# A tile shared by two batches earlier in the order, gates of nine tiles made together, and weight copies behind the exponentials

## The chip, the cores and the metric

The kernel runs on one core of one Trainium2 chip. A core has TensorE (matmuls and transposes), VectorE, ScalarE, GpSimd and SyncE (which here issues most DMAs), each with its own in-order queue of instructions, and they meet by semaphores only. The metric is the device time of one execution in microseconds; lower is better.

## The reference

Three stages follow one another: attention in a sliding window, a mixture of experts with one expert for each token, and a squared-ReLU network.

```python
# attention: q, k, v are (4, 8, 576, 64)
scores = scale * np.matmul(q, k.transpose(0, 1, 3, 2))
rel = pos[:, None] - pos[None, :]
scores = np.where((rel >= 0) & (rel < 64), scores, -1e9)
attn = softmax(scores)                       # exp, sum + 1e-9
x = np.matmul(attn, v)                       # -> (2304, 512): 4 batches of 576 rows
...
# experts: 8, with w1 (8, 512, 1024), w2 (8, 1024, 512)
logits = normalized(x) @ normalized(expert_emb).T / tau
expert_idx = np.argmax(logits, axis=1)
gate_w = softmax(logits)[arange, expert_idx]
out[mask] = gate_w[mask, None] * (np.maximum(x[mask] @ w1[e], 0.0) @ w2[e])
...
# second network: w_in (512, 2048), w_out (2048, 512)
r = np.maximum(x @ w_in, 0.0)
y = (s * (r * r) + b) @ w_out
```

## The kernel before

The 2304 rows of x are 18 tiles of 128, numbered 0 to 17. A batch has 576 rows, four and a half tiles, so tile 4 holds the last half of batch 0 and the first half of batch 1, and tile 13 the same of batches 2 and 3. Heads go in four pairs. A unit is one batch and one pair of heads; unit u = 4 * batch + pair, 16 in all. Q and K of a unit are loaded by SyncE, turned by TensorE in four pieces (K and Q, two heads each; `prep`, L220) and copied by ScalarE (both K pieces and the first Q piece) or VectorE (the second Q piece). There are eight sets of buffers for Q, K and V; unit u + 8 takes those of unit u once no step is left that uses u (`free`, L832).

Attention is 36 steps, numbered 0 to 35 here, in the order of the list `steps` (L825). Most steps take one pair of heads for two neighbouring tiles (`by_pair`); tiles 4 and 13, which lie in two batches, take steps of their own with two pairs of heads each (`alone`), and use four units at once. In the kernel before, tile 4 has steps 12 and 17, behind two pairs of heads of tiles 5 to 8 each time. A step n issues, on all engines in an order written out by hand: the scores (mask and products, TensorE, L251 and L210), the minimum and the subtraction (VectorE, L261 and L263), pieces of Q and K for later steps, the transposes of an earlier step's exponentials (`flip`, L271; two steps back, from step 31 on one), the exponential (ScalarE, L268), and then for a step one further back the product with V and the scaled output rows (`pv`, L279; L286 on TensorE, L289 to L295 on VectorE). How many pieces a step prepares (`prepare`, L885) follows from the units that the coming steps need: three pieces more than needed, less 2.4 for each step between, as far as the buffers are free. When a unit's last piece is turned, Q and K of the unit two further on are loaded, and V of the next as soon as its buffer is free.

When a tile's last pair of heads is done, `fin` (L673) starts its routing. GpSimd squares its rows and adds them up for the norm (`squares`, L399: one instruction over 512 elements and nine that halve; only tiles below 11). Later steps write the tile to DRAM, turn it (`route_turn`), and make its logits. For groups of tiles the table `ROUTED` (L792) then gives due steps, counted from the step of `fin`, for: ranks (`route_rank`, VectorE), count (`route_count`, TensorE), list (`route_list`, VectorE), `part` and `listed` for the tokens' numbers, and for the gates `route_norm` (one GpSimd root, L467), `route_gate` (L469: five VectorE instructions, an Exp on ScalarE, eight VectorE instructions), `part` again (the product Qv, VectorE, L458) and `listed` (one matmul a tile). In the kernel before, the groups are tiles 0 to 3 (gates at step 21), 4 to 8 (step 29) and 9 to 12 (step 32), each with ranks and gates of its own; the gates of the rest come after attention.

Work that is due is put down with `later` and one of four kinds, run in this order within a step (`run`, L808): TURN and WHOLE ahead of the exponential, HALF right behind it, BEHIND after the output rows.

When tiles up to 12 are counted, `first_weights` (L724) reads the number of the first full expert, loads four chunks of its first weight, and puts down a copy of each for steps 33 to 36. Such a copy (`split`, L85) is a rounding of 128 x 1024 on ScalarE (L86) and a difference on GpSimd (L87). `first_turn` (L742) at step 35 scales and turns the gathered rows for that expert. After attention come the experts, a planned order of the other engines around TensorE's fixed one, and the second network.

Of the kernel before, what the change touches and what calls it, by code (L numbers as in the profile page):

```python
# [20 lines left out]
def tile_kernel(ctx, tc, q, k, v, emb, tau, w1, w2, w_in, w_out, s_in, b_in, out, x_dram, y_dram, y0_dram, wi_dram, wo_dram):  # L21
# [14 lines left out]
    TL = 16  # L36
# [172 lines left out]
    def add(out, a, b):  # L209
        nc.tensor.matmul(out, a, b, start=False, stop=True, skip_group_check=True)  # L210
# [68 lines left out]
    def pv(slots, pT):  # L279
        po = ps1.tile([128, 4, D + 1], F32, tag="po", name="po")  # L280
        for s, (t, hp) in enumerate(slots):
            for h in range(2):
                for c in range(2):
                    rows = slice(64 * c, 64 * c + 64)
                    u, i = unit(t, hp, c)
                    nc.tensor.matmul(po[rows, 2 * s + h], pT[:, 2 * s + h, rows], vbufs[u][:, vslot(i), h], start=True, stop=True)  # L286
        with tc.high_priority(offset=PVP):
            rc = at3.tile([128, 4], F32, tag="rc", name="rc")
            nc.vector.tensor_scalar(rc, po[:, :, D], 1e-9, None, op0=ALU.add)  # L289
            nc.vector.reciprocal(rc, rc)  # L290
            (t0, h0), (t1, h1) = slots
            x = xs[t0].rearrange("p s (h q d) -> p s h q d", h=2, q=NP)
            x = x[:, :, :, h0] if t0 != t1 else x[:, 0, :, h0:h0 + 2].rearrange("p h q d -> p q h d")
            v4 = [128, 2, 2, D]
            nc.vector.tensor_tensor(x, po[:, :, :D].rearrange("p (s h) d -> p s h d", h=2),  # L295
                                    rc.rearrange("p (s h) -> p s h", h=2).unsqueeze(3).to_broadcast(v4), op=ALU.mult)
# [81 lines left out]
    def route_turn(t, lp=None):  # L378
        xw = rows_of(t)
        tp = ps3.tile([128, ND, 128], F32, tag="tp", name="tpx")  # L380
        for c in range(ND):
            nc.tensor.transpose(tp[:, c], xw[:, c * 128:(c + 1) * 128], ident)
        xt = (lp or at3).tile([128, ND, 128], F32, tag=f"xt{t}" if lp else "xt", name="xt")
        marks.append(nc.scalar.activation(xt, tp, AF.Copy))
        if t >= LATE:
            sq = (lp or at).tile([128, DM], F32, tag="sq", name="sq")
            if t >= TL:
                nc.vector.tensor_tensor_reduce(out=sq, in0=xw, in1=xw, scale=1.0, scalar=0.0,
                                               op0=ALU.mult, op1=ALU.add, accum_out=ss[:, t:t + 1])
            else:  # L390
                nc.scalar.activation(sq, xw, AF.Square, accum_out=ss[:, t:t + 1])
        return xt
# [6 lines left out]
    def squares(t):  # L399
        sq = x2p.tile([128, 1024], F32, tag="xh", name="sq")[:, :DM]  # L400
        nc.gpsimd.tensor_tensor(sq, rows_of(t), rows_of(t), op=ALU.mult)
        c = DM // 2
        while c >= 1:
            o = ss[:, t:t + 1] if c == 1 else sq[:, :c]
            nc.gpsimd.tensor_tensor(o, sq[:, :c], sq[:, c:2 * c], op=ALU.add)
            c //= 2
# [47 lines left out]
    def part(t0, t1, j0, j1):  # L454
        w, ts_ = j1 - j0, slice(t0, t1)
        vb_ = [128, t1 - t0, w, E * KT]
        Qv = rp2.tile(vb_, BF16, tag=f"Qv{w}", name="Qv")
        nc.vector.tensor_tensor(Qv, Q[:, ts_].rearrange("p t e k -> p t (e k)").unsqueeze(2).to_broadcast(vb_),  # L458
                                val[:, ts_, j0:j1].unsqueeze(3).to_broadcast(vb_), op=ALU.mult)
        return Qv  # L460

    def listed(t0, t1, j0, j1, Qv):
        for t in range(t0, t1):
            add(ls[:, j0:j1], lane[:, t], Qv[:, t - t0])

    def route_norm(t0, t1):
        nc.gpsimd.tensor_tensor(nrm[:, t0:t1], ss[:, t0:t1], half.to_broadcast([128, t1 - t0]), op=ALU.pow)  # L467

    def route_gate(t0, t1):  # L469
        n = t1 - t0  # L470
        ts_ = slice(t0, t1)

        sc = nrm[:, ts_]
        nc.vector.tensor_scalar(sc, sc, 1e-6, None, op0=ALU.add)
        nc.vector.reciprocal(sc, sc)
        scb = sc.unsqueeze(2).to_broadcast([128, n, E])
        L = rp2.tile([128, n, E], F32, tag="L", name="L")
        nc.vector.tensor_tensor(L, logit[:, ts_], scb, op=ALU.mult)
        mx = mxs[:, ts_]
        nc.vector.tensor_tensor(mx, mx, sc, op=ALU.mult)  # L480
        nc.vector.tensor_tensor(L, L, mx.unsqueeze(2).to_broadcast([128, n, E]), op=ALU.subtract)
        nc.scalar.activation(L, L, AF.Exp)
        gt = rp2.tile([128, n], F32, tag="gt", name="gt")
        nc.vector.tensor_reduce(gt, L, axis=AX.X, op=ALU.add)
        nc.vector.tensor_scalar(gt, gt, 1e-9, None, op0=ALU.add)
        nc.vector.reciprocal(gt, gt)
        for j in range(3):
            nc.vector.tensor_copy(val[:, ts_, 2 + j], gt)
            if j < 2:
                nc.vector.tensor_tensor(gt, gt, val[:, ts_, 2 + j], op=ALU.subtract)  # L490
# [182 lines left out]
    def fin(slots, pT):  # L673
        pv(slots, pT)
        t = slots[0][0]
        if slots[-1][1] < NP - 1:
            return
        ts_ = sorted({t for t, _ in slots})
        nt = len(ts_)
        if t < LATE:  # L680
            for k_ in ts_:
                squares(k_)

        def write():
            nc.sync.dma_start(x_dram[t * 128:(t + nt) * 128].rearrange("(s p) n -> p s n", p=128), xs[t])

        n = now[0]
        if n < len(steps):
            later(n + 1, write)
        else:  # L690
            write()
        if t == TL:
            return
        xts = {}

        def turned(t):
            xts[t] = route_turn(t)

        for j, k_ in enumerate(ts_):
            m = n + (0 if t >= LATE else j)  # L700
            later(m + 1, lambda k_=k_: turned(k_), TURN)
            later(m + 2, lambda k_=k_: route_logits(k_, xts[k_]), HALF)
        if ts_[-1] not in ROUTED:
            return
        (t0, t1), d = ROUTED[ts_[-1]]
        q = []
        later(n + d[0], lambda: route_rank(t0, t1), BEHIND)
        later(n + d[1], lambda: route_count(t0, t1))
        if t1 == TF:
            later(n + d[1], first_weights)  # L710
        later(n + d[2], lambda: route_list(t0, t1))
        later(n + d[3], lambda: q.append(part(t0, t1, 0, 2)))
        later(n + d[4], lambda: listed(t0, t1, 0, 2, q[0]))
        if t1 == TL:
            return
        later(n + d[5], lambda: route_norm(t0, t1))
        later(n + d[6], lambda: route_gate(t0, t1), BEHIND)
        later(n + d[7], lambda: q.append(part(t0, t1, 2, 5)), BEHIND)
        later(n + d[8], lambda: listed(t0, t1, 2, 5, q[1]))
        if t1 == TF:  # L720
            later(n + d[9], first_turn)
            later(n + d[4], first_rows)

    def first_weights():  # L724
        route_first(TF)
        rv = nc.values_load(efi[0:1, 0:1], engines=[mybir.EngineType.SP], min_val=0, max_val=E - 1)
        srcs.extend(expert_srcs(rv))
        w = sets[0] = []
        for c in range(ND):
            hl, do = load_part(srcs[c], nc.gpsimd)  # L730
            w.append(hl)
            later(now[0] + 2 + c, do, TURN)
        xa[:] = [x2p.tile([128, ND, 256], F32R, tag=t, name=t) for t in ("xh", "xl")]

    def first_rows():
# [39 lines left out]
    def first_part():  # L775
# [4 lines left out]
        for d in range(ND):  # L780
# [4 lines left out]
            if d == ND - 1:  # L785
# [3 lines left out]
    now = [0]  # L789
    TOACT = (("k", 0), ("k", 1), ("q", 0))  # L790

    ROUTED = {3: ((0, 4), (4, 5, 6, 7, 9, 10, 11, 12, 14)),  # L792
# [3 lines left out]
    LATE = 11  # L796
    xa = []
    xga = []
# [4 lines left out]
    TURN, WHOLE, HALF, BEHIND = range(4)  # L803

    def later(n, do, kind=WHOLE):
        todo.setdefault(n, []).append((kind, do))
# [11 lines left out]
    def by_pair(ts_, hps=range(NP)):  # L818
        return [((t, hp), (t + 1, hp)) for hp in hps for t in ts_]

    def alone(t, hp):
        return [((t, hp), (t, hp + 1))]


    steps = by_pair((0, 2)) + \  # L825
        by_pair((5, 7), (0, 1)) + alone(4, 0) + by_pair((5, 7), (2, 3)) + alone(4, 2) + \
        by_pair((9, 11)) + alone(13, 0) + alone(13, 2) + by_pair((14,)) + by_pair((16,))
    FIRST = {t: s[0][0] for s in steps for t, _ in s}
    used = [[(2 * t + c) // NW * NP + hp for t, hp in s for c in range(2)] for s in steps]
# [122 lines left out]
    with tc.manual_schedule(engines={mybir.EngineType.PE}):  # L952
        some(2)
        xts = [(t, route_turn(t, lp)) for t in range(TL, NTT)]
        with tc.issue_after(marks[-1].ins):
            for src in srcs[ND:]:
                hl, do = load_part(src, nc.gpsimd)
# [362 lines left out]
```

## Time and profile before

| | us |
|---|---|
| median of three runs | 868.21 |
| lowest and highest | 868.17, 868.93 |
| the profiled execution's own time | 870.09 |
| its span, first to last instruction | 868.3 |
| busy in the span: TensorE, VectorE, ScalarE, GpSimd | 791.0, 533.7, 383.3, 214.0 |
| last exponential of attention starts | 171.6 |

The profile is one execution. Its page gives the busy time of each engine, a picture of the span in 40 slices of 21.7 us, the chain that ended last and the costliest groups. Its views of single stretches give a line to each instruction (or run of equal ones): start, length, engine, source line, operation, what it writes and reads, and in brackets how long the engine stood idle before it and what ended that.

### The profile page before, as it was taken

The page shows a single profiled execution, that of the slowest core. Times are in us where ns is not written, and L with a number is a line of the kernel's source. Part 1 is how long each engine was busy: PE and PEld are TensorE (multiplying, and loading weights), DVE is VectorE, ACT ScalarE, POOL GpSimd, SP SyncE. Part 2 cuts the span into 40 slices and gives each one's busy share as a digit, 9 for nine tenths or more (in the row PEclk, how much of TensorE's full clock was granted, in tenths as well). Part 3 has the DMA queues.
Part 4 walks back from the last instruction along what each step waited for, and adds up shares of the span by engine and source line. Part 5 has one row for each costly group of instructions (what it writes and reads, how often), then busy time and mean ns, then how long its engine had stood idle before and what let it go on. Part 6 is the DMA issues. An engine that isn't in the chain of part 4 may idle for free. (4 is left out here: it accounts for less than half of the span.)

```text
span 868.3 us, 16641 instructions
## 1 busy us (share of the span) xinstructions
PE 791.0 (91%) x6494; PEld 726.7 (84%) x6494; DVE 533.7 (61%) x1093; ACT 383.3 (44%) x753; POOL 214.0 (25%) x265
## 2 busy tenths in 40 slices
PE   6898586467999999989989999999999999999997
PEld 5776475467999999879989999999999999999995
DVE  4886576666787766869946555566664544444442
ACT  6787353331453454544545444455544333333331
POOL 1163522343111334343501222222220110000000
PEclk9998687768999999999999999999999999999999
DMA  9876623312684977867565222233332211100000
GB/s 196 203 194 169 156 73 116 111 50 85 211 241 151 311 222 237 285 224 257 203 221 199 86 91 96 78 121 120 122 122 76 95 49 49 49 25 25 25 25 25
DMA packets 100641, 117.16 MB, mean 135 GB/s; under 512 B 38884, under 2 KB 72164, under 8 KB 100560
## 3 DMA queue, kind: packets, MB, share of 16 engines
q1 hardware_dynamic: 91072, 99.11, 38.0%
q0 software_dynamic: 3232, 10.24, 3.4%
q10 hardware_dynamic: 6256, 6.72, 2.3%
q8 instruction: 52, 0.85, 0.4%
q14 instruction: 29, 0.24, 0.1%
HBM read 91.52 MB, written 24.53 MB: 134 GB/s over the span
## 5 line engine op out<-in xcount | busy, mean ns | idle before, releaser
L125 PE MATMUL p<-xl,wh 128*128 128x256 f32 x576 | 162.4, 282 | 0.0
L125 PE MATMUL p<-xh,wh 128*128 128x256 f32 x576 | 162.2, 282 | 0.0
L125 PE MATMUL p<-xh,wl 128*128 128x256 f32 x576 | 161.7, 281 | 0.0
L1227 ACT ACTIVATE r<-p 128x256 f32<-128x256 f32 x144 | 55.5, 385 | 168.4 <-PE p L125 165.5
L1228 DVE SCALAR_TENSOR_TENSOR r<-r,s_bc 128x256 f32<-128x256 f32 x144 | 80.3, 560 | 79.5 <-ACT r L1227 79.3
L125 PE MATMUL p<-wh,gh 128*128 128x512 f32 x288 | 113.0, 392 | 0.0
L125 PE MATMUL p<-wl,gh 128*128 128x512 f32 x288 | 113.0, 392 | 0.0
L125 PE MATMUL p<-wh,gl 128*128 128x512 f32 x288 | 113.0, 392 | 0.0
L125 PEld LDWEIGHTS p<-xh,wh 128*128 128x128 f32 x576 | 108.8, 189 | 0.7
L125 PEld LDWEIGHTS p<-xl,wh 128*128 128x128 f32 x576 | 108.6, 189 | 0.8
L125 PEld LDWEIGHTS p<-xh,wl 128*128 128x128 f32 x576 | 109.0, 189 | 0.0
L1051 POOL TENSOR_TENSOR fl<-fl,fs 128x512 f32<-128x512 f32 x32 | 45.7, 1431 | 252.2 <-DVE fs L1050 202.1
L87 DVE TENSOR_TENSOR wl<-raw,wh 128x1024 fp32r<-128x1024 f32 x72 | 103.5, 1443 | 5.7 <-ACT wh L86 5.4
L86 ACT ACTIVATE wh<-raw 128x1024 fp32r<-128x1024 f32 x80 | 83.3, 1056 | 5.6 <-DMA raw<-wo_dram 2.4
L125 PE MATMUL p<-hh,wh 128*128 128x256 f32 (+5 forms) x256 | 78.7, 307 | 0.0
L125 PE MATMUL p<-hl,wh 128*128 128x256 f32 (+5 forms) x256 | 76.9, 301 | 0.0
L125 PE MATMUL p<-hh,wl 128*128 128x256 f32 (+5 forms) x256 | 76.9, 300 | 0.0
L1234 ACT ACTIVATE gh<-r,b_bc 128x256 fp32r<-128x256 f32 x144 | 72.7, 505 | 5.4 <-DVE r L1228 4.9
L1235 DVE SCALAR_TENSOR_TENSOR gl<-r,b_bc,gh 128x256 fp32r<-128x256 f32 x144 | 70.5, 489 | 3.1 <-ACT gh L1234 3.1
L1266 POOL DMA_INDIRECT out_dram<-o,ids x18 | 18.4, 1023 | 204.3 <-DVE o L1265 183.7
L131 PE MATMUL tp<-xh,wh 128*128 128x256 f32 (+6 forms) x288 | 54.8, 313 | 11.0 <-DVE hl L757 6.3
L125 PEld LDWEIGHTS p<-wh,gl 128*128 128x128 f32 x288 | 54.1, 188 | 12.2
(228 smaller groups left out, 1509.9 us busy)
## 6 DMA issues: line engine op xcount, KB each, us to landing
raw<-in_moe_w_dram SPq DMA_DIRECT2D x64, 512.0 KB, 5.4
raw<-y_dram SPq DMA_DIRECT2D x18, 512.0 KB, 5.1
vb<-in_v_dram SPq DMA_DIRECT2D x64, 128.0 KB, 3.8
fr<-in_moe_w_in_dram SPq DMA_DIRECT2D x16, 512.0 KB, 6.1
fr<-in_moe_w_out_dram SPq DMA_DIRECT2D x16, 512.0 KB, 3.7
k<-in_k_dram SPq DMA_DIRECT2D x32, 144.0 KB, 2.7
q<-in_q_dram SPq DMA_DIRECT2D x32, 144.0 KB, 3.6
x_dram<-xs SPq DMA_DIRECT2D x8, 512.0 KB
```

The lines of the kernel that those rows point to most:

```text
L86: a = nc.scalar.activation(hi, src, AF.Copy)
L87: return a.ins, le.tensor_tensor(lo, src, hi.bitcast(F32), op=ALU.subtract).ins
L125: nc.tensor.matmul(ps, a[x], b[y], start=first and j == 0, stop=last and j == 2)
L131: nc.tensor.matmul(ps, x, y, start=j == 0, stop=j == len(k) - 1)
L1051: nc.gpsimd.tensor_tensor(lf, lf, sg.bitcast(F32), op=ALU.mult)
L1227: nc.scalar.activation(r, ps, AF.Relu)
L1228: nc.vector.scalar_tensor_tensor(r, r, s_bc, r, op0=ALU.mult, op1=ALU.mult)
L1234: nc.scalar.activation(gh, r, AF.Identity, bias=b_bc)
L1235: nc.vector.scalar_tensor_tensor(gl, r, b_bc, gh.bitcast(F32), op0=ALU.add, op1=ALU.subtract)
L1266: nc.gpsimd.indirect_dma_start(out=out, out_offset=bass.IndirectOffsetOnAxis(ap=ids[:, k:k + 1], axis=0), in_=o, in_offset=None)
```

## The change

Three edits. Tile 4's steps move: after the first two pairs of heads of tiles 5 and 6 and before those of 7 and 8, so steps 10 and 15 in place of 12 and 17; tiles 7 and 8 now end at step 17 and carry the routing of tiles 4 to 8. Gates of tiles 0 to 3 are no longer made by themselves: root, gate, Qv and listing are made for tiles 0 to 8 together, the root at step 26, gate and Qv at 28 and the listing at 30; ranks, count, list and parts of tiles 4 to 8 come at steps 23, 24, 24, 25 and 26 (before: 23, 24, 25, 26 and 27); the gates of tiles 9 to 12 come at step 33 in place of 32. The copies of the first weights at steps 33 to 35 change their kind from TURN to BEHIND; the one at 36 stays.

```diff
@@ -702,7 +702,7 @@
         if ts_[-1] not in ROUTED:
             return
-        (t0, t1), d = ROUTED[ts_[-1]]
+        (t0, t1), gated_, d = ROUTED[ts_[-1]]
         q = []
         later(n + d[0], lambda: route_rank(t0, t1), BEHIND)
@@ -711,12 +711,12 @@
-        if t1 == TL:
+        if gated_ is None:
             return
-        later(n + d[5], lambda: route_norm(t0, t1))
-        later(n + d[6], lambda: route_gate(t0, t1), BEHIND)
-        later(n + d[7], lambda: q.append(part(t0, t1, 2, 5)), BEHIND)
-        later(n + d[8], lambda: listed(t0, t1, 2, 5, q[1]))
+        later(n + d[5], lambda: route_norm(*gated_))
+        later(n + d[6], lambda: route_gate(*gated_), BEHIND)
+        later(n + d[7], lambda: q.append(part(*gated_, 2, 5)), BEHIND)
+        later(n + d[8], lambda: listed(*gated_, 2, 5, q[1]))
@@ -729,7 +729,7 @@
             w.append(hl)
-            later(now[0] + 2 + c, do, TURN)
+            later(now[0] + 2 + c, do, BEHIND if now[0] + 2 + c < len(steps) else TURN)
@@ -789,10 +789,11 @@
-    ROUTED = {3: ((0, 4), (4, 5, 6, 7, 9, 10, 11, 12, 14)),
-              4: ((4, 9), (3, 4, 5, 6, 7, 8, 9, 10, 12)),
-              12: ((9, 13), (2, 3, 3, 3, 4, 4, 4, 4, 6, 7)),
-              15: ((13, 16), (2, 3, 3, 3, 4))}
+    ROUTED = {3: ((0, 4), None, (4, 5, 6, 7, 9)),
+              8: ((4, 9), (0, 9), (3, 4, 4, 5, 6, 6, 8, 8, 10)),
+              12: ((9, 13), (9, 13), (2, 3, 3, 3, 4, 4, 5, 5, 6, 7)),
+              15: ((13, 16), None, (2, 3, 3, 3, 4))}
@@ -823,7 +824,8 @@
     steps = by_pair((0, 2)) + \
-        by_pair((5, 7), (0, 1)) + alone(4, 0) + by_pair((5, 7), (2, 3)) + alone(4, 2) + \
+        by_pair((5,), (0, 1)) + alone(4, 0) + by_pair((7,), (0, 1)) + \
+        by_pair((5,), (2, 3)) + alone(4, 2) + by_pair((7,), (2, 3)) + \
         by_pair((9, 11)) + alone(13, 0) + alone(13, 2) + by_pair((14,)) + by_pair((16,))
```

## Rows read from the trace of the kernel before

**Rows 1.** The page's 40 slices: TensorE's granted clock in tenths of full speed.

```profile
PEclk9998687768999999999999999999999999999999
```

**Rows 2.** Windows: length, busy us of PE, PEld, DVE, ACT, POOL, clock, DMA share, GB/s.

```profile
93.50:107.20 13.70, 5.41 (x65) 4.63 (x68) 8.87 (x26) 5.97 (x13) 5.95 (x17) 0.50 0.50 127
...
203.00:440.00 237.00, 225.17 (x1649) 221.28 (x1647) 179.24 (x320) 105.73 (x175) 78.02 (x55) 1.00 0.70 226
```

**Rows 3.** Timeline of ScalarE: exponentials 17, 18, 21, 22, 29, 30 and 32 to 35.

```profile
68.93 0.63 ACT L268 ACTIVATE pe<-sm 128x512 f32<-128x512 f32 x1 [3.22 <-DVE sm L263]
75.34 0.62 ACT L268 ACTIVATE pe<-sm 128x512 f32<-128x512 f32 x1
...
87.78 0.62 ACT L268 ACTIVATE pe<-sm 128x512 f32<-128x512 f32 x1
...
101.77 0.63 ACT L268 ACTIVATE pe<-sm 128x512 f32<-128x512 f32 x1 [0.69 <-DVE sm L263]
...
129.76 0.65 ACT L268 ACTIVATE pe<-sm 128x512 f32<-128x512 f32 x1
...
137.34 0.63 ACT L268 ACTIVATE pe<-sm 128x512 f32<-128x512 f32 x1 [2.55 <-DVE sm L263]
...
146.87 0.63 ACT L268 ACTIVATE pe<-sm 128x512 f32<-128x512 f32 x1 [1.93 <-DVE sm L263]
...
156.72 0.63 ACT L268 ACTIVATE pe<-sm 128x512 f32<-128x512 f32 x1 [4.19 <-DVE sm L263]
...
164.68 0.64 ACT L268 ACTIVATE pe<-sm 128x512 f32<-128x512 f32 x1
...
171.58 0.62 ACT L268 ACTIVATE pe<-sm 128x512 f32<-128x512 f32 x1
```

**Rows 4.** Timeline of TensorE: three instructions that waited for VectorE.

```profile
101.79 0.43 PE L251 MATMUL spb<-mask,eye 64*64 64x256 bf16 x4 [10.32 <-DVE sm L263]
...
116.46 0.69 PE L286 MATMUL po<-vb,pT 128*64 128x65 f32 x16 [1.14 <-DVE xs L295]
...
157.56 1.13 PE L286 MATMUL po<-vb,pT 128*64 128x65 f32 x16 [6.12 <-DVE xs L295]
```

**Rows 5.** Timeline of VectorE: starts and ends of the three gates, and neighbours.

```profile
96.08 1.01 DVE L474 TENSOR_SCALAR nrm<-nrm 128x4 f32<-128x4 f32 x1 [6.98 <-POOL nrm L467]
...
100.33 0.69 DVE L261 TENSOR_REDUCE mn<-spb 128x4 f32<-128x512 f32 x1
...
125.70 0.42 DVE L295 TENSOR_TENSOR xs<-po,rc 128x256 f32<-128x256 f32 x1
...
133.09 0.17 DVE L474 TENSOR_SCALAR nrm<-nrm 128x5 f32<-128x5 f32 x1 [3.28 <-POOL nrm L467]
...
135.89 0.68 DVE L261 TENSOR_REDUCE mn<-spb 128x4 f32<-128x512 f32 x1
...
149.75 0.33 DVE L474 TENSOR_SCALAR nrm<-nrm 128x4 f32<-128x4 f32 x1
...
155.28 0.68 DVE L261 TENSOR_REDUCE mn<-spb 128x4 f32<-128x512 f32 x1
...
168.73 1.57 DVE L111 TENSOR_SCALAR xg<-xg,go 80x512 f32<-80x512 f32 x1
```

**Rows 6.** One line's instructions: the products Qv, shortest, median and longest in ns.

```profile
L458 DVE TENSOR_TENSOR Qv<-Q,val x9: 288/493/2573, 68.8 to 204.9; 128x256 bf16<-128x256 bf16 x2, 128x384 bf16<-128x384 bf16 x2, 128x480 bf16<-128x480 bf16 x2, 128x320 bf16<-128x320 bf16 x1
```

**Rows 7.** Timeline of GpSimd: two roots together, and the first weight's low part.

```profile
131.87 2.16 POOL L467 TENSOR_TENSOR nrm<-ss,half 128x5 f32<-128x5 f32 x2
...
152.61 2.33 POOL L87 TENSOR_TENSOR wl<-raw,wh 128x1024 fp32r<-128x1024 f32 x1 [2.51 <-ACT wh L86]
```

**Rows 8.** Timeline, ScalarE in step 18: copies of K pieces.

```profile
70.40 1.74 ACT L235 ACTIVATE kT<-tp 64x288 f32<-64x288 f32 x4 [0.84 <-PE tp L228]
```

**Rows 9.** TensorE's waits from 203 to 440 us, the largest: total, times, longest.

```profile
PE tp L131 <- DVE hl L757: 6.3, 7, 2.4
```

**Rows 10.** The page's DMA issues: KB each, median us from issue to landing.

```profile
q<-in_q_dram SPq DMA_DIRECT2D x32, 144.0 KB, 3.6
```

## The prediction

> **What bounds the kernel now.** I read the page's slices first: TensorE's granted clock is below full from the fourth slice to the tenth and full afterwards [rows 1]. The windows give it in numbers: from 203 to 440 us TensorE is busy for 225 of 237 us at clock 1.00, from 93.5 to 107.2 us for 5.4 of 13.7 us at 0.50, that is 1.2 of 2.4 GHz [rows 2]. What comes after attention is bound by TensorE's own work, so a microsecond won in attention should arrive at the end as one. Attention (to about 172 us) is bound by no engine's sum but by a round: scores on TensorE, minimum and subtraction on VectorE, next scores, through in-order queues. Whatever stands ahead of a step's two VectorE instructions delays the step. Third view: ScalarE makes one exponential a step, so their start times are the steps' clock [rows 3]. Steps 18 to 21 take (87.78 - 75.34) / 3 = 4.15 us each; I take that as an undisturbed step. Against it stand 14.0 us from exponential 21 to 22, 7.6 from 29 to 30, and 9.9, 8.0 and 6.9 from 32 to 35. Fourth view, TensorE's waits at those places: 10.32 us behind step 21 and 6.12 behind step 32, both released by VectorE [rows 4].
>
> VectorE's timeline tells why [rows 5]. It stood 6.98 us before the first instruction of the gate of tiles 0 to 3 (L474), waiting for GpSimd's root, which is queued behind squares of later tiles; the gate ran from 96.08 to 100.33, and behind it, in the same queue, waited step 22's minimum, hence the subtraction, the exponential, TensorE's next scores. The second gate (tiles 4 to 8) waited 3.28 us in the same way; its root ran at 131.87, right behind the squares of tile 10 [rows 7]. The third waited for no root, but its bf16 product Qv (L458) took 2.57 us, the longest of nine whose median is 0.49 [rows 6], while GpSimd made a weight's low part for 2.33 us [rows 7].
>
> **The change, part by part.**
>
> *First gate removed.* Root, gate (13 small VectorE instructions and an Exp), Qv and four matmuls for tiles 0 to 3 alone vanish. The step of 14.0 us becomes one of 4.15: 9.84 us, a little under TensorE's wait. The next step, at half clock until 107.2 us, gives back up to half of TensorE's 5.4 busy us; much of that lies beside other work, so I count 0.6. The squares that held the root stay, but nobody waits for them there. The transposed tiles of steps 19 to 21 (1, 2, 2) spread over 18 to 22 (1, 2, 0, 1, 1), the sum being equal. Gain 10.4 us, bounds 9.2 (two tiles' copies fall on the path, about 0.6 each) and 12.5 (all of the 2.7).
>
> *Steps 8 to 17 reordered.* With tile 4 at steps 10 and 15 instead of 12 and 17 the K/Q buffers of units 0 to 3 come free two steps sooner. By the rule in the code, six K/Q pieces made in a burst at step 18 become one more at 16, two more at 17 and three at 18. In that step ScalarE copied piece after piece, 0.44 us an instruction, two a piece (this row and two like it, ten instructions) [rows 8], and exponential 18 came 6.41 us after 17 [rows 3]. Three such pieces, 2.6 us, leave it. At step 17 two of them fill ScalarE's wait of 3.22 us for VectorE [rows 3]; at 16 one may cost 0.6. Gain 2.0 us, bounds 0 (moved, not hidden) and 3.2 (with the clock). Without that cover the 2.6 are paid where they go. Earlier, units 4 to 6 are made up to a step sooner, with three pieces at steps 5 and 7 and none at 9, which can't fall below its round of scores: -0.3, bounds -0.87 (a piece's copies) and +0.3. On GpSimd the squares of tiles 5 and 6 move a step sooner, of tile 4 two sooner, of 7 and 8 one later. On SP the V loads of units 8, 10 and 11 leave two steps sooner; TensorE waited for no load in these steps, so nothing for that.
>
> *List of tiles 4 to 8 right behind its ranks.* It moves from step 25 to 24. In step 25 pv waited 1.14 us for VectorE's output rows, which stood behind the list [rows 4]. That wait goes to step 24, where VectorE also has a Q copy: -0.5 us, bounds -1.14 and 0.
>
> *One gate for nine tiles, at step 28.* Its root, now at step 26, is issued ahead of the squares of tiles 9 and 10 (step 27), so the 3.28 us go. What is next late: VectorE begins after step 28's output rows, at 126.1 [rows 5], with GpSimd squaring until 131.87 [rows 7]. The five-tile gate took 133.09 to 135.89, 2.8 us, with GpSimd idle; the four-tile one 4.25 beside squares [rows 5]. Width hardly counts, so 4.6. Qv grows to 864 elements: from 0.49 at 256 to 480 about 1.1, with a hold 1.5. So minimum 29 starts at 132.3, exponential 29 at 133.75 (old 129.76); behind it are queued step 29's output rows and, on TensorE, scores 30: exponential 30 about 136.45 against 137.34. The stall is paid a step sooner and a little smaller: +0.9 us. Bounds -1.5 (2.4 us more of holds by GpSimd) and +3.4 (the whole excess, 7.58 - 4.15). The listing matmuls stay as many and go from steps 24 and 32 to 30.
>
> *Third gate a step later, first weights' copies behind the exponentials.* Step 32 no longer holds the gate: exponential 33 about 146.87 + 4.4 = 151.3 (old 156.72). But gate and Qv, 149.75 to 155.28 in the old order [rows 5], then stand behind step 33's output rows, and ScalarE makes the gate's Exp and behind it the first weight copy, so that GpSimd's low part again falls beside the gate's end and Qv. Behind Qv are queued VectorE's minimum 34 and, on TensorE, listing, pv and scores 35. Step 33 has the output rows of two steps, some 5.3 us, plus 5.5: exponential 34 at 162.1 (old 164.68, where ScalarE was late with the second copy). VectorE had used that lateness to run ahead, some 1.5 us which now show: exponential 35 at 162.1 + 6.9 + 1.5 = 170.5 against 171.58, +1.1 us. The second copy now holds the first scaling of gathered rows instead of the second, which took 1.57 [rows 5]. Bounds -2.3 (nothing won, one more hold of 2.33) and +3.4 (no hold at step 33).
>
> Sum: 10.4 + 2.0 - 0.3 - 0.5 + 0.9 + 1.1 = **13.6 us**. The profiled execution's own time is 870.1 us (span 868.3, 1.8 around it), which gives 856.5; that execution is 1.9 above the median of the runs, 868.2, and from the median it is 854.6.
>
> **A rule against the change.** Row first: L474 took 1.01 us beside GpSimd's squares and 0.17 with GpSimd idle [rows 5]. The Trainium skill, "SBUF — State Buffer", section "Who interferes with whom", has it that a VectorE instruction with two SBUF inputs contends with a GpSimd one that reads SBUF, and that the one that comes second is blocked for the other's whole length. The trace agrees, and the rule speaks against a wide gate beside squares and against copies behind exponentials; rival 2 is what that would cost.
>
> **Rivals.**
> 1. *The nine-tile gate is held as the first was.* If the root at step 26 still stands behind squares, VectorE waits up to 6.98 us again; the gate then runs beside nothing (-1.7), so 5.3 us are lost: 13.6 - 5.3 = 8.3, 859.9. For it: that queue held both old roots. Against: the squares of tiles 4 to 8 are issued six steps or more ahead of it. Chance 0.08.
> 2. *VectorE held by GpSimd at every turn.* 2.4 us more at step 28, a second hold of 2.33 at step 33 and one among the ranks of step 35: 13.6 - 7.0 = 6.6, 861.6. For it the rows above; against it that inside all three old gates most instructions kept their 0.2 us. Chance 0.10.
> 3. *Hidden anyway.* The expert stage would have to wait for something that doesn't move with it. The largest sum of TensorE's waits from 203 to 440 us is 6.3 us, for VectorE [rows 9], and none there is for a load. 868. Chance 0.03.
> 4. *Slower: Q and K not landed.* The new plan transposes unit 5's Q at step 7 and unit 6's K at step 8, a step sooner, two steps and one after their loads are issued. A Q load lands in 3.6 us in the median [rows 10], about one step. It decides once landing takes two steps, 8 us, in the loaded start; then each of three units holds TensorE some 6 us, 18 lost against 13.6 won: 872.6. Against it: no such wait now. Chance 0.03.
>
> **How the numbers follow.** Forecast 854.6, chance 0.76. The terms' bounds add up to 9.2 - 0.87 - 1.14 - 1.5 - 2.3 = 3.4 won and to 22.8; they don't fall together, so the range takes some two thirds of the lower side and most of the upper, since every stall that goes can free the clock too: 7.2 to 21.2 us, 847 to 861. It takes in rival 1; left out are rivals 2 to 4 and the forecast's far ends, below 0.2. A measurement of this kernel tells about 0.2%, 1.7 us. Faster 0.94 (forecast, rivals 1 and 2), same 0.03 (3), slower 0.03 (4).
>
> **What would show it.** Right: no wait for a root near step 21, exponential 22 about 4 us after 21 and no half clock there; one gate whose Qv has 864 elements, with TensorE waiting 3 to 4 us near steps 29 and 30; exponentials 17 and 18 under 5 us apart; the long step from 33 to 34 instead of 32 to 33; the stage after attention as long as before. Wrong: a root behind squares again, gate instructions over 1 us in a row, TensorE waiting for a K or Q load, or a longer stage after attention.

## The result, and the profile after

The changed kernel takes 854.77 us, the median of its runs (854.39 to 857.90); the kernel before took 868.19 beside it (866.84 to 868.93). The ratio over all executions of both is 0.9855, with an interval of 0.9829 to 0.9882: 1.45% faster (the two medians alone give 0.9845). The forecast was 854.6. The profiled execution of after took 857.9 us with a span of 856.2, against 870.1 and 868.3.

ScalarE's timeline, exponentials 18, 21, 22, 29 to 35 of the changed kernel, answers to [rows 3]:

```profile
73.56 0.63 ACT L268 ACTIVATE pe<-sm 128x512 f32<-128x512 f32 x1
...
84.65 0.63 ACT L268 ACTIVATE pe<-sm 128x512 f32<-128x512 f32 x1
88.13 0.63 ACT L268 ACTIVATE pe<-sm 128x512 f32<-128x512 f32 x1
...
116.26 0.63 ACT L268 ACTIVATE pe<-sm 128x512 f32<-128x512 f32 x1 [2.48 <-DVE sm L263]
119.14 0.62 ACT L268 ACTIVATE pe<-sm 128x512 f32<-128x512 f32 x1
126.97 0.62 ACT L268 ACTIVATE pe<-sm 128x512 f32<-128x512 f32 x1
132.19 0.63 ACT L268 ACTIVATE pe<-sm 128x512 f32<-128x512 f32 x1 [2.32 <-DVE sm L263]
137.15 0.62 ACT L268 ACTIVATE pe<-sm 128x512 f32<-128x512 f32 x1
147.51 0.63 ACT L268 ACTIVATE pe<-sm 128x512 f32<-128x512 f32 x1 [2.15 <-DVE sm L263]
156.19 0.62 ACT L268 ACTIVATE pe<-sm 128x512 f32<-128x512 f32 x1
```

From 21 to 22 it now takes 3.48 us where it took 13.99. The long steps are 28 to 29, 30 to 31, and 33 to 35. Set against the starts of before, the steps say where the time went (all from ScalarE's timelines, us):

| step | before | after | difference |
|---|---|---|---|
| 18 | 75.34 | 73.56 | -1.78 |
| 21 | 87.78 | 84.65 | -3.13 |
| 22 | 101.77 | 88.13 | -13.64 |
| 23 | 106.53 | 91.16 | -15.37 |
| 28 | 125.16 | 108.46 | -16.70 |
| 30 | 137.34 | 119.14 | -18.20 |
| 31 | 141.68 | 126.97 | -14.71 |
| 35 | 171.58 | 156.19 | -15.39 |
| end of the span | 868.3 | 856.2 | -12.1 |

The page's line of the clock answers to [rows 1]; the windows of after answer to [rows 2], with the same columns, the first over the stretch that was at half clock, the second over the nine-tile gate.

```profile
PEclk9999976679999999999999999999999999999999
```

```profile
93.50:107.20 13.70, 9.56 (x183) 7.97 (x183) 12.53 (x34) 6.85 (x13) 2.20 (x2) 1.00 0.49 88
107.20:124.00 16.80, 12.65 (x207) 11.14 (x205) 10.91 (x31) 6.77 (x15) 9.15 (x21) 0.74 0.17 63
```

The stretch from 93.5 to 107.2 us went from clock 0.50 to 1.00, and TensorE was busy 9.56 us of it where it was 5.41. (The two windows hold different steps: before, most of it was the wait; after, steps 24 to 27 run there.) The clock falls later instead, from the nine-tile gate on, while TensorE stands behind VectorE.

VectorE's timeline, the nine-tile gate at step 28 (first instruction, a held one, Qv and the minimum behind it), then a held one of the third gate, its Qv, and the second scaling of gathered rows; this answers to [rows 5] and [rows 6]:

```profile
109.24 0.16 DVE L474 TENSOR_SCALAR nrm<-nrm 128x9 f32<-128x9 f32 x1
...
111.60 1.06 DVE L490 TENSOR_TENSOR gt<-gt,val 128x9 f32<-128x9 f32 x1
...
113.72 1.18 DVE L458 TENSOR_TENSOR Qv<-Q,val 128x864 bf16<-128x864 bf16 x1
114.83 0.68 DVE L261 TENSOR_REDUCE mn<-spb 128x4 f32<-128x512 f32 x1
...
142.82 2.33 DVE L488 CAST val<-gt 128x4 bf16<-128x4 f32 x1
...
145.59 0.56 DVE L458 TENSOR_TENSOR Qv<-Q,val 128x384 bf16<-128x384 bf16 x1
...
154.44 0.47 DVE L111 TENSOR_SCALAR xg<-xg,go 80x512 f32<-80x512 f32 x1
```

GpSimd's, the joint root, two squares around the gate and the first weight's low part, answers to [rows 7]:

```profile
93.51 1.83 POOL L467 TENSOR_TENSOR nrm<-ss,half 128x9 f32<-128x9 f32 x1
106.83 1.04 POOL L401 TENSOR_TENSOR sq<-xs 128x512 f32<-128x512 f32 x1 [11.49 <-DVE xs L295]
...
111.59 1.04 POOL L401 TENSOR_TENSOR sq<-xs 128x512 f32<-128x512 f32 x1
...
142.77 2.34 POOL L87 TENSOR_TENSOR wl<-raw,wh 128x1024 fp32r<-128x1024 f32 x1 [7.34 <-ACT wh L86]
```

No gate waits for a root: the joint one ends at 95.34, the gate starts at 109.24. The small instruction held for 1.06 us started within 0.01 us of a square 1.04 long, and the one held for 2.33 us 0.05 after the start of a low part 2.34 long.

TensorE's, a wait for K (behind exponential 20), the wait of step 24, and steps 29 and 30 behind the gate; this answers to [rows 4]:

```profile
82.31 0.44 PE L228 MATMUL tp<-ident,k 96*128 96x96 f32 x3 [0.82 <-DMA k<-in_k_dram]
...
98.97 0.69 PE L286 MATMUL po<-vb,pT 128*64 128x65 f32 x16 [2.07 <-issue]
...
116.28 0.43 PE L251 MATMUL spb<-mask,eye 64*64 64x256 bf16 x4 [4.15 <-DVE sm L263]
...
118.40 0.92 PE L210 MATMUL rt<-Qv,lhot 128*128 128x96 bf16 x9
119.26 2.74 PE L210 MATMUL rt<-enT,xt 128*64 128x8 f32 x48
```

The 10.32 us of [rows 4] are gone; 4.15 are new. The last line, 48 logit matmuls of step 30, comes back below.

### The profile page after: what moved, and what is told of

The parts are those of the page before. It is cut to its first block, busy times and chain, and to the rows that moved or that the text cites. A ratio compares the mean times of both kernels' runs of the same rounds, so it can differ in the third digit from the quotient of the medians.

```text
span 856.2 us, 16632 instructions
## 1 busy us (share of the span) xinstructions
PE 790.7 (92%) x6494; PEld 728.2 (85%) x6494; DVE 530.0 (62%) x1079; ACT 382.8 (45%) x752; POOL 214.6 (25%) x264
## 5 line engine op out<-in xcount | busy, mean ns | idle before, releaser
L131 PE MATMUL tp<-xh,wh 128*128 128x256 f32 (+6 forms) x288 | 56.8, 323 | 12.5 <-DVE hl L757 5.4
L125 PEld LDWEIGHTS p<-wh,gl 128*128 128x128 f32 x288 | 54.1, 188 | 12.2
```

Source lines behind the costliest of these rows:

```text
L125: nc.tensor.matmul(ps, a[x], b[y], start=first and j == 0, stop=last and j == 2)
L131: nc.tensor.matmul(ps, x, y, start=j == 0, stop=j == len(k) - 1)
```

## Experiments

Each ratio is to the kernel before, run on the same chip, with its 95% interval. Besides the total I read ScalarE's timeline, since single steps show what an edit does to its place.

### Was it the wait for the root?

The theory: VectorE's wait for a root queued behind squares was the cost, and no gate has to be joined to lose it. The rival: the four-tile gate itself, beside squares, was. Three kernels take parts of the change alone.

**reorder_only**: the kernel before with the new order of steps alone.

```diff
-        by_pair((5, 7), (0, 1)) + alone(4, 0) + by_pair((5, 7), (2, 3)) + alone(4, 2) + \
+        by_pair((5,), (0, 1)) + alone(4, 0) + by_pair((7,), (0, 1)) + \
+        by_pair((5,), (2, 3)) + alone(4, 2) + by_pair((7,), (2, 3)) + \
-              4: ((4, 9), (3, 4, 5, 6, 7, 8, 9, 10, 12)),
+              8: ((4, 9), (3, 4, 5, 6, 7, 8, 9, 10, 12)),
```

> The kernel before with the new order of steps alone; every group keeps gates of its own. Theory (the cost is VectorE's wait for a root that stands behind squares): with this order only the squares of tiles 5, 6 and 4 stand ahead of the first root at step 20, those of 7 and 8 come behind it, so the root runs near 85 us instead of 95, the first gate hardly waits, and to some 2 us from the spread K/Q pieces come about 7: 859 us. Rival (the cost is the gate's own 13 instructions and product): only the 2 to 3 us from the spread pieces, 866 us, and exponential 22 still 10 us or more behind 21.

Measured: 862.57 us, 0.9894 (0.9859 to 0.9928). GpSimd's first root and VectorE's two gates in it:

```profile
84.47 1.05 POOL L467 TENSOR_TENSOR nrm<-ss,half 128x4 f32<-128x4 f32 x1
```

```profile
87.14 0.23 DVE L474 TENSOR_SCALAR nrm<-nrm 128x4 f32<-128x4 f32 x1
...
122.22 0.17 DVE L474 TENSOR_SCALAR nrm<-nrm 128x5 f32<-128x5 f32 x1 [4.12 <-POOL nrm L467]
```

The new order brings the squares forward, so the first root is done before the gate asks for it, and the step from 21 to 22 takes 5.39 us with the gate still in it. The second gate still waits 4.12.

**early_roots**: the kernel before, with only the two roots issued earlier (steps 17 and 27, ahead of squares, for 20 and 28).

```diff
-    ROUTED = {3: ((0, 4), (4, 5, 6, 7, 9, 10, 11, 12, 14)),
-              4: ((4, 9), (3, 4, 5, 6, 7, 8, 9, 10, 12)),
+    ROUTED = {3: ((0, 4), (4, 5, 6, 7, 9, 7, 11, 12, 14)),
+              4: ((4, 9), (3, 4, 5, 6, 7, 7, 9, 10, 12)),
```

> The kernel before with one change: the roots of the first two groups fall due earlier, at step 17 instead of 20 and at step 27 instead of 28, ahead of the squares they stood behind. No gate is removed. Theory (wait for the root): 7.0 us at the first gate and 3.3 at the second come back, 858 us; exponentials 21 to 22 about 7 us apart instead of 14. Rival (the gate's own work, which stays): 866 us or more.

Measured: 861.08 us, 0.9876 (0.9842 to 0.9910). GpSimd's root and VectorE's first gate in it:

```profile
60.21 1.05 POOL L467 TENSOR_TENSOR nrm<-ss,half 128x4 f32<-128x4 f32 x1
```

```profile
89.94 0.16 DVE L474 TENSOR_SCALAR nrm<-nrm 128x4 f32<-128x4 f32 x1
```

Nothing is removed here but the waits, and 21 to 22 falls from 13.99 to 6.47 us (88.71 to 95.18); 28 to 31, with the second gate, falls from 16.52 to 13.78. The step from 22 to 23 stays as long as it was, 4.77 us at granted clock 0.50, against 4.76 at 0.50 in the kernel before and 3.03 at 1.00 in the changed kernel. So here the clock behind the first gate did not come back with the wait. In reorder_only, also without the wait but with the gate, it was 0.67 and the step took 3.65 us; in full it came back where the gate is gone too.

**join_only**: the changed kernel with the old order of steps and the old handling of the first weights, so the joint gate alone.

```diff
-        by_pair((5,), (0, 1)) + alone(4, 0) + by_pair((7,), (0, 1)) + \
-        by_pair((5,), (2, 3)) + alone(4, 2) + by_pair((7,), (2, 3)) + \
+        by_pair((5, 7), (0, 1)) + alone(4, 0) + by_pair((5, 7), (2, 3)) + alone(4, 2) + \
-              8: ((4, 9), (0, 9), ...
-              12: ((9, 13), (9, 13), (2, 3, 3, 3, 4, 4, 5, 5, 6, 7)),
+              4: ((4, 9), (0, 9), ...
+              12: ((9, 13), (9, 13), (2, 3, 3, 3, 4, 4, 4, 4, 6, 7)),
-            later(now[0] + 2 + c, do, BEHIND if now[0] + 2 + c < len(steps) else TURN)
+            later(now[0] + 2 + c, do, TURN)
```

> The changed kernel without its other two edits: old order of steps, old kind of the weight copies, third gate at step 32; only the gates of tiles 0 to 8 are made together at step 28. Theory: the first gate's 10.4 us of the prediction, -0.5 for the list and about -1 to +1 at the wide gate: 858 us. Rival (without the new order the squares of tile 4 still hold the root, or the wide gate stalls as the first one did): 862 us or more. If the three edits add up, this and reorder_only together bring more than the changed kernel; if both remove the same wait, they don't add up.

Measured: 861.51 us, 0.9874 (0.9840 to 0.9908); 21 to 22 takes 3.78 us, 28 to 29 7.53.

So 1.1, 1.2 and 1.3% come from three edits that share one effect, the lost wait for the first root. In the step from 21 to 22 their gains don't add: 8.6 us with the new order, 10.2 with the joint gate, and 10.5 in the changed kernel, which has both. In the totals they nearly do: 1.06 and 1.26% against 2.06% for no_behind below, which is these two edits together, on the same chip. Where the totals make up what the step doesn't is open; other stretches differ as well (join_only reaches exponential 21 at 89.69 us, the kernel before at 87.78, reorder_only at 86.27). The rival explains only the smaller part: with the gates kept, losing the waits is worth 1.24%, where the whole change gives 1.45. But the first gate itself has a price beside it: from 21 to 23 early_roots takes 11.24 us and the changed kernel 6.51.

### The third edit, and its parts

**no_behind**: the changed kernel without the third edit. **no_behind_2** is the same kernel in a later comparison, and **after_again** the changed kernel unaltered, beside it.

```diff
-            later(now[0] + 2 + c, do, BEHIND if now[0] + 2 + c < len(steps) else TURN)
+            later(now[0] + 2 + c, do, TURN)
-              12: ((9, 13), (9, 13), (2, 3, 3, 3, 4, 4, 5, 5, 6, 7)),
+              12: ((9, 13), (9, 13), (2, 3, 3, 3, 4, 4, 4, 4, 6, 7)),
```

> The changed kernel without its third edit: copies of the first weights ahead of the exponentials again, third gate at step 32 again. Theory (term of 1.1 us in the prediction): 1 us slower than the changed kernel, 855.8 us, with the long step from 32 to 33 again, 9 to 10 us, and exponential 35 about 1 us later against exponential 31. Rival (the gate's stall only moves): 854.8 us. Rival the other way (copies late delay the first expert): faster than the changed kernel.

> The changed kernel without its third edit, beside the changed kernel. Prediction's theory: 1 us slower than the changed kernel. Theory from the trace of no_behind: there the product Qv of the third gate began 0.17 us ahead of GpSimd's low part and took 0.56 us, in the kernel before it began 0.17 us behind it and took 2.57; if VectorE comes first again, 2 to 4 us faster than the changed kernel, and if it comes second, 0 to 1 us slower.

> The changed kernel once more, on the same chip as the next three, which are compared with it. Ratio to the kernel before 0.985, as measured before; its third edit taken out (run no_behind) gave 0.979 on another chip. If the third edit costs time, the next run is 0.3 to 0.6% below this one; if that was the chip, both are equal.

Measured: no_behind 854.03 us, 0.9794 (0.9761 to 0.9826); no_behind_2 853.37, 0.9822 (0.9798 to 0.9846); after_again 858.59, 0.9866 (0.9836 to 0.9896). In the shared comparison the kernel without the third edit is the faster one, with intervals that overlap by 0.001; its first run lies below the changed kernel's 0.9855 with intervals apart. VectorE's Qv of the third gate and GpSimd's first low part in no_behind:

```profile
137.53 0.56 DVE L458 TENSOR_TENSOR Qv<-Q,val 128x384 bf16<-128x384 bf16 x1
```

```profile
137.70 2.59 POOL L87 TENSOR_TENSOR wl<-raw,wh 128x1024 fp32r<-128x1024 f32 x1 [2.85 <-ACT wh L86]
```

The same two as in [rows 6] and [rows 7], with the same 0.17 us between their starts, but the other way round: here Qv came first and took 0.56 us, and GpSimd paid with 2.59 for 2.33; in the kernel before GpSimd came first (152.61 against 152.78), and Qv took 2.57. The line of the kernel before:

```profile
152.78 2.57 DVE L458 TENSOR_TENSOR Qv<-Q,val 128x384 bf16<-128x384 bf16 x1
```

The hold that the third edit was to remove depended on who came first, and the earlier edits had already turned it. The expectation of no_behind, 1 us slower, missed; its rival the other way came.

**gate32** keeps the copies behind the exponentials and puts the third gate back to step 32; **copies_turn** takes back the other half, with the copies ahead and the gate at 33; **behind_only** is the kernel before with the copies behind.

```diff
 gate32, on the changed kernel
-              12: ((9, 13), (9, 13), (2, 3, 3, 3, 4, 4, 5, 5, 6, 7)),
+              12: ((9, 13), (9, 13), (2, 3, 3, 3, 4, 4, 4, 4, 6, 7)),
 copies_turn, on the changed kernel
-            later(now[0] + 2 + c, do, BEHIND if now[0] + 2 + c < len(steps) else TURN)
+            later(now[0] + 2 + c, do, TURN)
 behind_only, on the kernel before
-            later(now[0] + 2 + c, do, TURN)
+            later(now[0] + 2 + c, do, BEHIND if now[0] + 2 + c < len(steps) else TURN)
```

> The changed kernel with the third gate back at step 32, ahead of the first weight copy, while the copies stay behind the exponentials. Theory (the third edit's loss is that its gate and the copy's low part meet at step 33): no VectorE instruction of the gate over 0.7 us, step 32 to 33 about 8 us, 33 to 34 about 7 instead of 10.4, 2 us or more faster than the changed kernel. Rival (the loss is the late copies, which then block VectorE in step 35 and delay the first expert): as fast as the changed kernel, and the hidden layer's first wait for a weight longer than 1.0 us.

> The changed kernel with the third gate at 33 but the copies ahead of the exponentials, the fourth cell beside the changed kernel (33, behind), no_behind (32, ahead) and gate32 (32, behind). Theory (what counts is which of the gate and GpSimd's low part comes first): the low part is over before the gate begins at step 33, no gate instruction over 0.7 us, steps 32 to 34 about 2 us shorter than in the changed kernel, about 856 against its 858. Rival (the third gate's place is what counts): as slow as the changed kernel.

> The kernel before with the copies of the first weights at steps 33 to 35 behind the exponentials and nothing else changed; the third gate stays at 32 and so meets no copy. Theory (in the kernel before the product Qv came 0.17 us behind the low part and was held for 2 us): Qv of the third gate about 0.56 us, step 32 to 33 about 7.8 us instead of 9.9, and part of the 2 us given back by step 35, where the second copy's low part comes late: 867 us, 1 us faster. Rival (copies ahead cost the exponentials their time): 2 us or more faster. Rival the other way: slower.

Measured: gate32 855.88 us, 0.9844 (0.9819 to 0.9870); copies_turn 854.66, 0.9774 (0.9752 to 0.9796); behind_only 872.98, 0.9991 (0.9976 to 1.0005), no difference. Since these edits act between exponentials 32 and 35, that stretch tells them apart better than totals (us, from ScalarE's timelines):

| third gate at | copies | kernels | 32 to 35 |
|---|---|---|---|
| 32 | ahead, Qv second | before, reorder_only, early_roots, best | 24.7, 24.7, 24.5, 24.5 |
| 32 | ahead, Qv first | join_only, no_behind, no_behind_2, separate | 22.7 in all four |
| 32 | behind | gate32, behind_only | 24.1, 23.5 |
| 33 | behind | after, after_again, gate29 | 24.0, 24.4, 21.9 |
| 33 | ahead | copies_turn | 20.9 |

With the copies behind, no kernel but gate29 takes less than 23.5 us, even where Qv is not held (0.56 us in both kernels of the third line). So gate32 missed its theory: no gate instruction was held and 32 to 34 came as expected (7.83 and 7.33 us), but the 2 us were not won. The loss stands in the last step: 34 to 35 takes 8.7 to 9.1 us in all five traces with the copies behind and 6.9 to 7.4 in all nine others. In gate32 the second low part meets VectorE there, in a 128 x 2 instruction of step 35 (L509, 0.16 us in no_behind) that stands ahead of the scaling of the gathered rows:

```profile
150.22 2.20 DVE L509 TENSOR_TENSOR go<-li 128x2 f32<-128x2 f32 x1
```

```profile
149.99 2.41 POOL L87 TENSOR_TENSOR wl<-raw,wh 128x1024 fp32r<-128x1024 f32 x1 [4.97 <-ACT wh L86]
```

This is the rival's late copy that blocks VectorE in step 35; in behind_only the next instruction (L510) is held for 2.25 us. The rival's other sign tells nothing: the hidden layer waits 1.2 us for a weight in gate32, in the changed kernel and in the kernel before. With the copies ahead the stretch is 22.7 where Qv comes first, and 20.9 in the one kernel with the gate at 33, as copies_turn's theory had it. (Gate29 went from 32 to 33 at clock 1.00, in 3.58 us; the changed kernel at 0.51, in 4.96.) The last kernel of the table, on VectorE (third gate's first instruction and Qv) and on GpSimd (first two low parts):

```profile
140.86 0.16 DVE L474 TENSOR_SCALAR nrm<-nrm 128x4 f32<-128x4 f32 x1
...
143.72 0.56 DVE L458 TENSOR_TENSOR Qv<-Q,val 128x384 bf16<-128x384 bf16 x1
```

```profile
138.57 2.34 POOL L87 TENSOR_TENSOR wl<-raw,wh 128x1024 fp32r<-128x1024 f32 x1 [2.85 <-ACT wh L86]
144.04 2.51 POOL L87 TENSOR_TENSOR wl<-raw,wh 128x1024 fp32r<-128x1024 f32 x1 [3.13 <-ACT wh L86]
```

The gate falls between two low parts: one ends at 140.91, the next starts at 144.04, over the end of a Qv that came first, and there it is GpSimd that pays, 2.51 us. In the changed kernel the first copy follows the gate's Exp on ScalarE, and the low part falls into the gate at 142.77.

### Where the joint gate stands, and whether joining matters

**gate29**: the changed kernel with gate and Qv a step later, and the listing two steps later, at 32.

```diff
-              8: ((4, 9), (0, 9), (3, 4, 4, 5, 6, 6, 8, 8, 10)),
+              8: ((4, 9), (0, 9), (3, 4, 4, 5, 6, 6, 9, 9, 12)),
```

> The changed kernel with the nine-tile gate and its product one step later, at 29 (listing at 32). Theory (the trace of the changed kernel: with the gate at 28 TensorE waits ahead of scores 30 and then has step 30's 48 logit matmuls, at half clock, still to do, so steps 28 to 31 took 18.5 us; with a gate at 29 that work lies beside the gate, and early_roots took 13.8): steps 28 to 31 about 15 us, 3 us faster than the changed kernel. Rival (the gate's length is what counts, wherever it stands): 18 us and no gain.

Measured: 850.21 us, 0.9784 (0.9759 to 0.9808), against 0.9866 for the changed kernel in the same comparison; the two intervals stand apart. From 28 to 31 it takes 14.73 us; the changed kernel took 18.51 and 18.82. TensorE's timeline in gate29, step 30's logits and the scores behind the gate:

```profile
114.12 1.57 PE L210 MATMUL rt<-enT,xt 128*64 128x8 f32 x48
...
119.67 0.43 PE L251 MATMUL spb<-mask,eye 64*64 64x256 bf16 x4 [3.47 <-DVE sm L263]
```

The kernel before had the same run in the same place, beside its gate:

```profile
130.09 1.57 PE L210 MATMUL rt<-enT,xt 128*64 128x8 f32 x48
```

With the gate at 29, the 48 matmuls stand ahead of TensorE's waiting scores and run beside the gate at granted clock 1.00, 1.57 us. With it at 28 they stand behind those scores and run after the gate, at 0.50, 2.74 us. Two things go with it: the nine listing matmuls, 0.92 us behind the gate in the changed kernel, leave the stretch, and gate and Qv take 4.5 us (113.75 to 118.21) for 5.6, since their start falls otherwise against GpSimd's squares and no instruction of the gate is held over 0.35 us. How much of the 3.8 to 4.1 us each is worth was not taken apart. Some 2 us more of gate29's gain stand in the table above, from 32 to 35. The stretch from 28 to 31 repeats: 14.73 us in best too, which also has the gate at 29, and 17.2 to 18.8 in all seven traces with it at 28.

**best** joins gate29 and no_behind. **separate** is best with the two gates kept apart, at 21 and 29, their roots issued early (17 and 26).

```diff
 separate, on the changed kernel, beside the edit of no_behind
-    ROUTED = {3: ((0, 4), None, (4, 5, 6, 7, 9)),
-              8: ((4, 9), (0, 9), (3, 4, 4, 5, 6, 6, 8, 8, 10)),
+    ROUTED = {3: ((0, 4), (0, 4), (4, 5, 6, 7, 9, 7, 11, 12, 14)),
+              8: ((4, 9), (4, 9), (3, 4, 4, 5, 6, 6, 9, 9, 12)),
```

> The changed kernel with the nine-tile gate at step 29 and without its third edit (copies ahead of the exponentials, third gate at 32). Theory (two separate losses): the 7 us of gate29 and the 4 us of no_behind against the changed kernel add up, ratio to the kernel before about 0.974. Rival (both shift the same later stall, or the meeting of the product Qv with GpSimd's low part falls the other way at the new time): no better than gate29, 0.978.

> As best, but the gates of tiles 0 to 3 and 4 to 8 are made apart again, at steps 21 and 29, each root ahead of the squares it stood behind (steps 17 and 26). It tells what joining the gates is worth once no gate waits for a root. Theory (joining saves only the first gate's own instructions): exponential 21 to 22 about 6 us, as in early_roots, instead of 3.5, so 2 us slower than best, and still over 8 us faster than the kernel before. Rival (joining was the gain): 6 us or more slower than best.

Measured: best 854.26 us, 0.9777 (0.9757 to 0.9798); separate 854.44, 0.9794 (0.9768 to 0.9820). The first is no faster than gate29: its expected sum missed, and the hold is back in it, as it is in reorder_only and early_roots; VectorE's Qv and GpSimd's low part in best:

```profile
135.53 2.57 DVE L458 TENSOR_TENSOR Qv<-Q,val 128x384 bf16<-128x384 bf16 x1
```

```profile
135.36 2.33 POOL L87 TENSOR_TENSOR wl<-raw,wh 128x1024 fp32r<-128x1024 f32 x1 [2.31 <-ACT wh L86]
```

And separate isn't told apart from best by its time. But the traces differ: 21 to 22 takes 5.03 us against 3.45, 22 to 23 4.70 at clock 0.64 against 3.05 at 1.00, and all of 21 to 31 takes 41.47 us against 38.47 (38.85 in gate29). Against that, separate reached exponential 21 1.4 us sooner (85.02 against 86.42), and Qv came first in it (137.33 against 137.50), 1.8 us less from 32 to 35. So making the gates together, apart from the wait it removes, gains some 3 us in that stretch of one trace each, and was not shown to gain in the total. By ratio copies_turn, best and gate29 (0.9774, 0.9777, 0.9784, in two comparisons) are the fastest, 0.7 to 0.9% ahead of the changed kernel and not told apart; gate29 with copies_turn's edit wasn't run.

## Why the prediction was right

The forecast of 854.6 us held to 0.2 us. That closeness is luck, since the first terms were too small and one had the wrong sign. The sum to exponential 35 was 13.6 us won; the profiled execution won 15.39 there. The terms in turn:

- **First gate removed**, +10.4 predicted; 12.2 measured (the difference goes from -3.13 at exponential 21 to -15.37 at 23). The mechanism held, and early_roots shows that the wait was most of it, 7.5 us. The size was off by 0.7 in the step itself, which takes 3.48 us and not 4.15, and by 1.1 in the clock: I counted 0.6 for the step at half clock, and the step from 22 to 23 went from 4.76 us at 0.50 to 3.03 at 1.00.
- **Steps 8 to 17 reordered**, +2.0 - 0.3 predicted; 1.78 by exponential 18, 3.13 by 21. One trace measures this poorly: exponential 18 stands at 75.3 to 76.3 us in the four traces with the old order, and at 73.6 to 74.9 in the ten with the new one. As an edit by itself it was undersized, by a path that the prediction left out: in reorder_only the moved squares alone free the first root. Together with the joint gate that gain in step 21 is the first term's, not a second one.
- **List closer to its ranks**, -0.5 predicted. TensorE stood 2.07 us in step 24 where it stood 1.14 in step 25; the row calls it issue, while VectorE's output rows, behind ranks and list in its queue, ended at 98.86, just ahead of the matmul at 98.97. Yet the steps from 23 to 28 gained 1.33 us in all. This isn't the list's doing: early_roots, with the list where it was, takes 17.53 us for them, the changed kernel 17.30, the kernel before 18.63.
- **Nine-tile gate at 28**, +0.9 predicted; -2.0 measured from 28 to 31. **This is the step that failed.** Up to exponential 30 it was about right (+1.5 measured; the gate and Qv 5.6 us from 109.24 to 114.83, where 4.6 and 1.5 were counted; two instructions of 1.06 and 0.56 us among those of 0.2). It stopped there, as if the steps behind were unaffected. Step 30's matmuls, which had lain beside the old gate, came out from under it, and 30 to 31 took 7.83 us for 4.34. Gate29 bears this out: with the same work beside the gate the stretch is 3.8 to 4.1 us shorter, about 1.1 of it from a gate that was held less.
- **Third edit**, +1.1 predicted; +0.7 measured from exponential 31 to 35, with 4.96, 10.36 and 8.68 us for the three steps from 32 where 4.4, 10.8 and 8.4 were worked out. So against the old kernel its size was about right. But that isn't what the edit is worth: with it undone on the changed kernel, 32 to 35 is 1.3 to 1.7 us shorter. The prediction took the 2.57 us hold of [rows 6] for a fixed cost that only moving the gate removes. It wasn't one, and this is the second step that failed: with the earlier edits in place Qv comes first anyway (no_behind), so that hold was already gone, and the edit's price in the last step, 8.7 us for 6.9, stayed.
- **After attention**, 0 predicted. In the profiled execution 3.3 us came back: from exponential 35 to the end of the span it took 700.0 us against 696.7. But the changed kernel's other profiled execution took 696.7, and two of no_behind 696.6 and 693.3, so executions of one kernel differ as much as that. What sets it is open. The granted clock of the stretch goes along with part of it only: 0.97 in the executions of 700.0 and 696.6 us, 0.98 in those of 696.7 and 693.3.

So the total came out of errors of opposite sign: up to exponential 28 the first three terms won 16.7 us where 11.6 were predicted, 5.1 more; the nine-tile gate gave 2.9 less than its term and the third edit 0.4 less, which leaves 15.4 where the sum was 13.6. After attention the profiled execution gave back 3.3, so its span is 12.1 shorter, and its own time 12.2 (870.1 to 857.9); the medians differ by 13.4.

The rivals: the joint root did not queue behind squares (rival 1). VectorE was held at both gates, 1.06 and 0.56 us at 28 and 2.33 at 33, but the sum had counted as much: 6.1 us for gate and Qv at 28, and one hold at 33. Of the 7.0 us that rival 2 priced on top, one instruction of 0.73 us is seen in step 35 (L509, 0.16 in the kernel before). The gain was not hidden (rival 3): all but the 3.3 us above arrived. Of rival 4 one wait of 0.82 us for K is seen, behind exponential 20 and not in steps 7 or 8.

The rule of the Trainium skill ("SBUF — State Buffer", section "Who interferes with whom"), that the one that issues first has the shared access for its whole length, was the right one to weigh, and I used only half of it. The page also states "Issue order, not op shape, decides who blocks". These runs agree: a Qv of one shape takes 0.56 or 2.57 us, by 0.17 us in the order of the starts. Read so, [rows 6] and [rows 7] show a coincidence that an earlier edit can turn, not a property of that step. The row that the prediction set beside the rule was not its best witness: L474 has one tensor for input, where the rule speaks of two, and its 0.17 us was not beside an idle GpSimd, since two roots ran from 131.87 to 134.03 [rows 7]. Why some instructions with one input are held too, as the conversion of 2.33 us was, no run here takes apart.

## What to carry to other kernels

When an engine waits for a small result, look first at what is queued ahead of its maker: issuing the roots earlier, two numbers in a table, gave 1.24% where the whole change gave 1.45 (the change without its third edit gave 1.8 to 2.1). A long stall of one engine should stand where the others still have independent work ahead of the instruction that waits for it; follow it past the first late step to the work that comes out from under it. Where VectorE and GpSimd start within a few tenths of a microsecond of each other, price both orders, because an unrelated edit upstream decides which one it will be.

## What the runs showed of the hardware

A start 0.17 us earlier or later decided between 0.56 and 2.57 us for the same VectorE instruction; the loss is lopsided, since GpSimd as the second lost only 0.26 us (2.59 for 2.33), when 0.39 us of Qv were left. Very small instructions pay the same: a conversion of 128 x 4 took 2.33 us, and an addition of 128 x 2 2.20 (0.16 in no_behind).

GpSimd's root grew with its width although it is tiny: 1.05 us at 128 x 4 and 1.83 at 128 x 9. And the clock came back in full only where the gate went with the wait: in the kernel before TensorE stood 10.32 us at the first gate and had 0.50 in the step behind (4.76 us); in early_roots it still stood 2.81 us and had 0.50 there (4.77 us); in the changed kernel, without a gate at that place, it had 1.00 (3.03 us).
